# Attention stages of a four-layer kernel: one PSUM bank set aside for transposes, products of queries and keys drained by one copy, and small work moved to GpSimd

## The chip, the cores and the metric

The kernel runs on one NeuronCore of one Trainium2 chip. The metric is the device time of one execution in microseconds (us); the median of several runs is given, and the profile shows one further execution. Engines are named as in the profile: PE is TensorE (matrix products; PEld are its weight loads), DVE is VectorE, ACT is ScalarE, POOL is GpSimd, SP is SyncE, which here issues most of the DMAs.

## The reference

Four layers in turn on x of shape (1, 2048, 640): a Fourier layer, an attention layer, and both once more. Each adds its result to x.

```python
def _A_ref(x, seq_re, seq_im, hid_re, hid_im):        # Fourier layer
    a = einsum("bsd,ed->bse", x, hid_re); b = einsum("bsd,ed->bse", x, hid_im)
    return einsum("ts,bse->bte", seq_re, a) - einsum("ts,bse->bte", seq_im, b)

def _B_ref(x, wqkv, wo):                              # attention, 32 heads of 20, window of 256
    q, k, v = heads(x @ wqkv)
    scores = where(0 <= i - j < 256, q @ k.T * 20 ** -0.5, -1e9)
    return (softmax(scores) @ v) @ wo

x = x + _A_ref(layernorm(x), ...);  x = x + _B_ref(layernorm(x), ...)
x = x + _A_ref(layernorm(x), ...);  x = x + _B_ref(layernorm(x), ...)
```

Inputs and output are fp32. The kernel makes its large products from fp16 parts: each operand is a high part (the fp32 value rounded to fp16) and a low part (what is left, rounded again), and a product takes three matmuls, high by high, high by low and low by high.

## The kernel before

The program runs four stages: a spectral stage (Fourier layer), an attention stage, and both again. The change is in the attention stages; in the profile the first runs from about 602 to 1187 us, the second from about 1743 us to the end.

An attention stage goes through 256 steps `g`: 8 blocks of 256 queries, and 32 steps in a block, each for one tile of 128 queries and one pair of heads. What a step does is shifted against `g` by lags, counted in steps:

- at `g`, `scores(g)`: PE multiplies queries by keys into the bank `sp`; DVE masks it (COPY_PREDICATED, L1048) and takes the row maxima (TENSOR_REDUCE, L1052, into `m`; four steps share one `m`).
- at `HAND_LAG` (5) after the first step of each four, at the end of the step, `hand_on(n)`: the four steps' maxima are scaled and split into high and low parts in the tile `tops` (ACT L1058, then DVE L1059); four PE transposes put them into a PSUM bank, and two small ACT copies (L1067) put them into rows of `qs`, the stacked queries, so that the second product subtracts the maxima.
- at `KEY_LAG` (7), `by_key(g)`: PE multiplies keys by queries into the bank `tp`; ACT takes the sigmoid form of the exponential (L1088, into `ptq`); for every second pair POOL applies two triangular masks (L1093, L1095).
- at `VALUE_LAG` (12), `values(n)`: 32 PE matmuls of probabilities by values into `pv`, and one ACT copy. At `BACK_LAG` (14), `back(n)`: two PE transposes, DVE's division, and POOL's split (L1139, L1140) into `os`.

The banks `sp` and `tp` are single: a step's scores wait for the step before to be reduced.

Between these lies **filler work**, run by `run_fill`, which spends a credit of nanoseconds in each step (the rate is what is left of the filler over the steps that are left, times a factor `FILL` by the step's place among four). A filler unit is a generator that yields after each matmul. Kinds: products that make the next block's queries and keys (`Projections.qk`, 15 matmuls of 256 columns), values (`proj_v`) and outputs (`out_tile`, 15 of 320 columns), and **turns**: five transposes of a normed row tile or an output tile (`turned`), drained by one copy (ACT L952 for high parts, DVE L950 for low parts). A turn is taken by `step` in the middle of a product, after its seventh matmul, or by `run_fill` where no product is ready. `flush` runs to the end the units that the next block needs.

Products, turns and transposed maxima all take their bank from `new_f`, which hands out three banks in a fixed round: two of the pool `pf` and one of `p3`. A bank is free once the engine that drains it is done. A product of queries and keys is drained by two instructions, in line: ACT writes the high part (L328), then DVE reads the bank again, subtracts the high part, and writes the low part (L329); a DMA then stores both. Values are drained by ACT (L822), outputs by DVE (L877).

A layer norm in filler time (`norm_steps`, stepped by `slow_step`) runs on DVE, and ends with the normed tile `lny` (L147); `split` then has ACT make the high part (L159) and POOL the low part (L160) of `xs`.

All PE instructions of an attention stage keep the order of the code (`tensor` adds an order edge). The other engines' queues are put in order by the framework's scheduler, each engine runs its queue strictly in that order, and a waiting instruction holds all behind it.

Of the kernel before, what the change touches and what calls it, by code (L numbers as in the profile page):

```python
# [26 lines left out]
QB = 256  # L27
# [15 lines left out]
HAND_LAG = 5  # L43
KEY_LAG = 7
VALUE_LAG = 12
BACK_LAG = 14
# [12 lines left out]
def body(ctx: ExitStack, tc: tile.TileContext, x_in, cmat, whid, wqkv, wo, out):  # L59
# [18 lines left out]
    tops = [pers.tile([P, 4, 2, DH + 44], F16, name=f"tops{k}") for k in range(2)]  # L78
# [39 lines left out]
    def norm_steps(xs, ys):  # L118
# [26 lines left out]
        for k, x in enumerate(xs):  # L145
            y = keep.tile([P, D], F32, tag="lny", name="lny", bufs=2)
            normed[0] = nc.vector.tensor_scalar(y, x, mv[:, k, 0:1], g[:, k:k + 1],  # L147
                                                op0=OP.subtract, op1=OP.mult).ins
            ys.append(y)
            yield  # L150
# [142 lines left out]
    class Projections:  # L293


        def __init__(self):
# [7 lines left out]
            self.new_f = new_f  # L304
# [8 lines left out]
        def qk(self, b, w, ct):  # L313
            pf = self.new_f()
# [13 lines left out]
            nc.scalar.activation(t[:, 0], pf[:, :QB], AF.Copy, scale=down)  # L328
            nc.vector.scalar_tensor_tensor(t[:, 1], pf[:, :QB], down, t[:, 0], op0=OP.mult, op1=OP.subtract)  # L329
# [428 lines left out]
    def attention(layer, proj, dst, final):  # L758
        with ExitStack() as st:
# [14 lines left out]
            third = [0]  # L774
# [8 lines left out]
            proj.new_f = new_f  # L783
# [118 lines left out]
            def next_norm(i, x3):  # L902
                ys = []
                yield from norm_steps([x3], ys)
# [37 lines left out]
            def turned(xs, k, o, d0=0, d1=ND):  # L942
                pt = new_f()
# [43 lines left out]
            def step(u):  # L987

# [7 lines left out]
                if u.n % 15 == 7 and ns and not u.turn:  # L996
                    t = next_unit(True)
                    while t and step(t):
                        pass
                return True  # L1000

            def run_fill(ns):
                credit[0] += ns
                while credit[0] > 0:
                    if unit[0] is None:
                        unit[0] = next_unit(False) or next_unit()
                        if unit[0] is None:
                            credit[0] = 0.0
                            break
# [43 lines left out]

            def hand_on(n):

                b, q = divmod(n, NP // 2)
                m, hl = TOP.pop(n), tops[n % 2]
                nc.scalar.activation(hl[:, :, :, 0], m, AF.Copy, scale=-1.0 / M_UP)  # L1058
                nc.vector.scalar_tensor_tensor(hl[:, :, :, 1], m, -1.0 / M_UP, hl[:, :, :, 0], op0=OP.mult, op1=OP.subtract)  # L1059
                hp = new_f().bitcast(F16)[:, :4 * P].rearrange("p (a b) -> p a b", a=4)  # L1060
                for k in range(4):
                    transpose(hp[:66, k], hl[:, k].rearrange("p a b -> p (a b)")[:, :66], idh)
                for pi in range(2):
                    rs = slice(64 * pi, 64 * pi + 2)
                    o = QS[b][rs, 2 * q:2 * q + 2].rearrange("r p (i t) -> r i p t", i=2)
                    t = hp[rs].rearrange("r (i p) t -> r i p t", i=2)
                    nc.scalar.activation(o, t, AF.Copy)  # L1067
# [122 lines left out]
            for g in range(NS):  # L1190
# [12 lines left out]
                if g < NG and r == VALUE_LAG:  # L1203
# [7 lines left out]
                    if b == NBQ - 1 and not final:  # L1211
                        hidden = Hidden(xu_d)
                        hidden.load()
                        for k in range(2):
                            hidden.fetch(k)
                            fill.append(Unit(g + NEXT_STEPS[k], hidden.stage(k, None, new_f), "next", NG + k))
# [17 lines left out]
            while unit[0] is not None or fill or slow:  # L1234
                now[0] += 1
                run_fill(1600)
# [37 lines left out]
```

## Time and profile before

| | us |
|---|---|
| median of 3 runs | 2340.88 (2326.55 to 2344.01) |
| the profiled execution, its own time | 2334.45 |
| its span in the profile | 2332.7 |
| busy, of the span: PE / DVE / ACT / POOL | 92% / 73% / 55% / 51% |
| first and second attention stage | about 585 and 590 |

The engines run beside each other, so busy shares do not add up; the engine that is busy nearly all the time is PE, and what it waits for is what can be gained. The prediction is worked out against the profiled execution, 2334.45 us, which lies 0.3% below the median.

### The profile page before, as it was taken

To read this page: it belongs to the slowest core of one execution; us is meant where nothing else is said; L and a number is where in the kernel's file an instruction comes from. 1 tells how busy PE (TensorE), PEld (TensorE's weight loads), DVE (VectorE), ACT (ScalarE), POOL (GpSimd) and SP (SyncE) were. 2 spreads that over 40 slices of the span, in tenths; PEclk is the share of its full clock that TensorE was granted. 3 is DMA by queue.
4 is the path that set the end of the run, shared out by engine and by line. 5 is a ranking of instruction groups with operands and counts; after the bars stand their busy time and mean duration, and the time that the engine had idled before them with its cause. 6 is when DMAs were issued, how large, how long until landed. Compare 5 with 4: busy or idle time off the path is not lost.

```text
span 2332.7 us, 54695 instructions
## 1 busy us (share of the span) xinstructions
PE 2145.9 (92%) x21985; PEld 1504.6 (64%) x21985; DVE 1707.3 (73%) x3633; ACT 1290.8 (55%) x2248; POOL 1196.4 (51%) x1453
## 2 busy tenths in 40 slices
PE   7999899989899889999989999999898899999997
PEld 5667566667566666666556777777665666666664
DVE  7887969777668777776757858584767777677674
ACT  5334443333477677776764434334326677667675
POOL 5676757656134344443446858585642333334333
PEclk9999999999999999999999999999999999999999
DMA  5854646364421332232414535363642322232120
GB/s 185 290 208 155 217 144 208 133 226 132 133 79 44 95 90 64 59 96 70 155 70 154 193 130 191 128 214 148 227 116 70 87 60 67 67 87 75 54 76 24
DMA packets 187603, 292.93 MB, mean 126 GB/s; under 512 B 13908, under 2 KB 120660, under 8 KB 178004
## 3 DMA queue, kind: packets, MB, share of 16 engines
q1 hardware_dynamic: 157108, 223.55, 31.1%
q10 hardware_dynamic: 30240, 65.88, 7.6%
q8 instruction: 172, 2.82, 0.5%
q14 instruction: 83, 0.68, 0.1%
HBM read 202.51 MB, written 86.87 MB: 124 GB/s over the span
## 4 chain that ended last, share of the span: by engine, by line
PE 61%; DVE 21%; ACT 8%; DMA 5%; issue 4%; POOL 1%; SPq 0%; ACTq 0%; DVEq 0%; POOLq 0%
PE pf L112 26%; PE y L112 9%; PE pv L112 7%; PE z L112 6%; PE x L112 6%; DVE cc L481 5%; PE sp L112 4%; ACT ptq L1088 4%; DVE m L1052 3%; PE tp L112 3%; DVE sp L1048 2%; ACT qs L1067 2%; DVE res L504 1%; DVE early L329 1%; DVE lnst L125 1%
## 5 line engine op out<-in xcount | busy, mean ns | idle before, releaser
L112 PEld LDWEIGHTS <-cc 128*128 128x128 f16 x5376 | 527.6, 98 | 244.9 <-issue 37.8
L1088 ACT ACTIVATE ptq<-tp,shift,alpha 128x768 f32<-128x768 f32 (+2 forms) x512 | 487.0, 951 | 159.5 <-PE tp L112 134.1
L112 PEld LDWEIGHTS <-big 128*128 128x128 f16 x4320 | 411.6, 99 | 160.5 <-issue 47.7
L1093 POOL TENSOR_SCALAR_AFFINE_SELECT ptq<-ptq 128x512 f32<-128x512 f32 x224 | 144.3, 644 | 526.9 <-ACT ptq L1088 523.7
L1052 DVE TENSOR_REDUCE m<-sp 128x2 f32<-128x512 f32 (+1 forms) x512 | 345.1, 674 | 16.2
L112 PE MATMUL pf<-early,big 128*128 128x256 f16 x2400 | 316.2, 276 | 17.0 <-DVE early L329 16.9
L1048 DVE COPY_PREDICATED sp<-mask,sp 128x256 f32<-128x256 int32 x448 | 190.9, 426 | 162.3 <-PE sp L112 152.6
L478 ACT ACTIVATE cc<-cs 128x512 f16<-128x512 f32 x256 | 152.2, 623 | 256.6 <-POOL cs L471 99.9
L112 PE MATMUL y<-zc,cc 128*128 128x320 f16 x1728 | 268.2, 303 | 14.6 <-DVE pf L504 14.6
L112 PE MATMUL pf<-big 128*128 128x320 f16 x1680 | 241.7, 302 | 12.9 <-DVE early L250 7.4
L481 DVE SCALAR_TENSOR_TENSOR cc<-cs,cc 128x512 f16<-128x512 f32 x256 | 233.9, 929 | 3.6 <-ACT cc L478 3.6
L1095 POOL TENSOR_SCALAR_AFFINE_SELECT ptq<-ptq 128x512 f32<-128x512 f32 x256 | 164.9, 644 | 104.7 <-ACT ptq L1088 104.7
L481 DVE SCALAR_TENSOR_TENSOR cc<-cq,cc 128x512 f16<-128x512 f32 x192 | 203.4, 1060 | 0.0
L112 PE MATMUL pv<-ptq,v 128*32 128x128 f32 (+1 forms) x3840 | 185.9, 333 | 0.0
L112 PE MATMUL z<-zc,cc 128*128 128x320 f16 x1152 | 178.1, 299 | 5.6 <-DVE res L504 5.6
L112 PE MATMUL x<-zc,cc 128*128 128x320 f16 x1152 | 180.7, 301 | 0.0
L112 PE MATMUL sp<-ks,qs 62*128 62x256 f16 (+1 forms) x1792 | 153.9, 250 | 26.2 <-DVE m L1052 22.3
L112 PE MATMUL pf<-big,early 128*128 128x320 f16 x960 | 159.2, 301 | 7.8 <-DVE x L877 4.3
L112 PE MATMUL tp<-qs,ks 62*128 62x128 f16 x2688 | 151.0, 218 | 11.1 <-ACT ptq L1088 10.5
L1067 ACT ACTIVATE qs<-pf 2x512 f16<-2x512 f16 x224 | 131.2, 586 | 52.8 <-PE pf L112 47.2
L112 PE MATMUL pf<-bo,ot 128*128 128x320 f16 x840 | 146.3, 302 | 8.4 <-DVE x L877 3.7
L112 PEld LDWEIGHTS <-ks 62*128 62x128 f16 x3008 | 117.3, 95 | 54.2 <-issue 22.6
(140 smaller groups left out, 3383.8 us busy)
## 6 DMA issues: line engine op xcount, KB each, us to landing
cq<-in_cmat_dram SPq DMA_DIRECT2D x64, 1024.0 KB
accd<-res ACTq DMA_DIRECT2D x96, 320.0 KB
res<-accd SPq DMA_DIRECT2D x96, 320.0 KB
x<-x2d SPq DMA_DIRECT2D x64, 320.0 KB
qkd<-early SPq DMA_DIRECT2D x160, 128.0 KB
ks<-qkd SPq DMA_DIRECT2D x108, 160.0 KB
qs<-qkd SPq DMA_DIRECT2D x84, 160.0 KB
x2d<-res ACTq DMA_DIRECT2D x32, 320.0 KB
```

Source lines behind the costliest of these rows:

```text
L112: i = getattr(nc.tensor, what)(*args, **kw)
L125: nc.vector.bn_stats(st[:, h], x[:, h * 320:(h + 1) * 320])
L329: nc.vector.scalar_tensor_tensor(t[:, 1], pf[:, :QB], down, t[:, 0], op0=OP.mult, op1=OP.subtract)
L478: nc.scalar.activation(cc[m][:, 0], f, AF.Copy, scale=C_UP)
L481: nc.vector.scalar_tensor_tensor(cc[m][:, 1], f, C_UP, cc[m][:, 0], op0=OP.mult, op1=OP.subtract)
L504: marks["dve"] = nc.vector.scalar_tensor_tensor(o, z, Y_DOWN, f, op0=OP.mult, op1=OP.add).ins
L1048: nc.vector.copy_predicated(sp[:, :, 2 * P:3 * P], mask[:, None, :].to_broadcast([P, 2, P]), far)
L1052: topped[0] = nc.vector.tensor_reduce(TOP[g // 4][:, g % 4], sp[:, :, c0:3 * P], axis=AX.X, op=OP.max).ins
L1067: nc.scalar.activation(o, t, AF.Copy)
L1088: nc.scalar.activation(q[:, h:h + 2, a0 + first:a0 + 3], tp[:, :, first * P:3 * P].rearrange("p a (b c) -> p a b c", c=P), AF.Sigmoid, bia ...
L1093: nc.gpsimd.affine_select(out=q[:, :, a0], in_=q[:, :, a0], pattern=[[0, 4], [-1, P]], base=0, channel_multiplier=1, compare_op=OP.is_gt, ...
L1095: ins = nc.gpsimd.affine_select(out=q[:, :, a0 + 2], in_=q[:, :, a0 + 2], pattern=[[0, 4], [1, P]], base=0, channel_multiplier=-1, compare ...
```

## The change

Six edits, all for the attention stages (`Projections.qk` and `norm_steps` are also called at the end of the spectral stages):

1. `new_f` gives products the two banks of `pf` alone. The bank `p3` is kept for turns and transposed maxima, through `new_turn`.
2. A product of queries and keys is drained by one ACT copy to an fp32 tile `qf` in SBUF; POOL makes the high part (a cast) and the low part (a subtraction) from it.
3. The maxima are scaled, cast and subtracted on POOL (`part_tops`, three small instructions), in the middle of step `HAND_LAG`, now 4; `hand_on` at the end of that step only transposes; the two ACT copies are written in the code one and two steps later (`copy_tops`).
4. `norm_steps` of an attention stage writes the normed tile on POOL.
5. `VALUE_LAG` and `BACK_LAG` go from 12 and 14 to 13 and 15. The order of `FILL` moves with `VALUE_LAG`.
6. Turns are no longer taken inside products: `turn_unit` runs one whole turn ahead of the filler in the step of `hand_on` and in the step before it (two steps in four), and after the last scores in each step.

```diff
-HAND_LAG = 5
+HAND_LAG = 4
 KEY_LAG = 7
-VALUE_LAG = 12
-BACK_LAG = 14
+VALUE_LAG = 13
+BACK_LAG = 15
...
-            normed[0] = nc.vector.tensor_scalar(y, x, mv[:, k, 0:1], g[:, k:k + 1],
+            normed[0] = eng.tensor_scalar(y, x, mv[:, k, 0:1], g[:, k:k + 1],
...
-            nc.scalar.activation(t[:, 0], pf[:, :QB], AF.Copy, scale=down)
-            nc.vector.scalar_tensor_tensor(t[:, 1], pf[:, :QB], down, t[:, 0], op0=OP.mult, op1=OP.subtract)
+            f = keep.tile([P, QB], F32, tag="qf", name="qf", bufs=2)
+            nc.scalar.activation(f, pf[:, :QB], AF.Copy, scale=down)
+            nc.gpsimd.tensor_copy(t[:, 0], f)
+            nc.gpsimd.tensor_tensor(t[:, 1], f, t[:, 0], op=OP.subtract)
...
-            def new_f():
-
-                third[0] += 1
-                if third[0] % 3 or not in_turn[0]:
-                    return pf_.tile([P, 512], F32, tag="f", name="pf", bufs=2)
-                return p3.tile([P, 512], F32, tag="f", name="pf")
+            def new_turn():
+
+                return p3.tile([P, 512], F32, tag="f", name="pt") if in_turn[0] else new_f()
...
-                yield from norm_steps(x2s, ys)
+                yield from norm_steps(x2s, ys, nc.gpsimd)
...
-                pt = new_f()
+                pt = new_turn()
...
-                if u.n % 15 == 7 and ns and not u.turn:
-                    t = next_unit(True)
-                    while t and step(t):
-                        pass
+            def turn_unit():
+                t = next_unit(True)
+                while t and step(t):
+                    pass
...
-                        unit[0] = next_unit(False) or next_unit()
+                        unit[0] = next_unit(False)
...
+            def part_tops(n):
+
+                m, hl = TOP.pop(n), tops[n % 2]
+                u = sb.tile([P, 4, 2], F32, tag="u", name="u", bufs=2)
+                nc.gpsimd.tensor_scalar(u, m, -1.0 / M_UP, None, op0=OP.mult)
+                nc.gpsimd.tensor_copy(hl[:, :, 0:66:64], u)
+                nc.gpsimd.tensor_tensor(hl[:, :, 1:66:64], u, hl[:, :, 0:66:64], op=OP.subtract)
+
             def hand_on(n):
 
-                b, q = divmod(n, NP // 2)
-                m, hl = TOP.pop(n), tops[n % 2]
-                nc.scalar.activation(hl[:, :, :, 0], m, AF.Copy, scale=-1.0 / M_UP)
-                nc.vector.scalar_tensor_tensor(hl[:, :, :, 1], m, -1.0 / M_UP, hl[:, :, :, 0], op0=OP.mult, op1=OP.subtract)
-                hp = new_f().bitcast(F16)[:, :4 * P].rearrange("p (a b) -> p a b", a=4)
+                hl = tops[n % 2]
+                hp = new_turn().bitcast(F16)[:, :4 * P].rearrange("p (a b) -> p a b", a=4)
...
+                if (g - HAND_LAG) % 4 in (0, 3) or g >= NG + HAND_LAG:
+                    turn_unit()
                 run_fill(max(rate, 400) * FILL[(g - VALUE_LAG + 2) % 4])
```

What it does to the order of PE, at the end of a step that hands maxima on, is seen at two places of the first attention stage. Before, step 89 (`bo`, `ot`: an output product; `os`: a turn of an output tile; `tops_78`: the maxima); the turn stands in the middle of a product, and the maxima directly behind it, each in a bank of its own:

```order
L112 MATMUL pf<-bo_66,ot 128x320
L112 LDWEIGHTS os
L112 MATMUL pf<-idh,os 128x128
...
L112 LDWEIGHTS tops_78
L112 MATMUL pf<-idh,tops_78 66x128
...
L112 LDWEIGHTS qs
```

After the change, step 96, the first of a block, in which no filler has credit:

```order
L112 MATMUL tp<-qs,ks 128x128
L112 LDWEIGHTS os
L112 MATMUL pt<-idh,os 128x128
...
L112 LDWEIGHTS tops_78
L112 MATMUL pt<-idh,tops_78 66x128
...
L112 LDWEIGHTS qs
```

The turn has moved to right behind the second product `tp`, and both now write the same bank, `pt`. Of the 128 times that maxima are handed on, 41 have a turn ahead of them in the same step (37 before, and then in other banks); in 12 of the 41 nothing stands between, in the other 29 there is a product's share of 1280 to 3840 columns, 2240 in the middle one.

On POOL, in the first attention stage, the new work (`qf` and `early`: a product's copy and its parts; `u` and `tops`: the maxima) stands between the masks of `ptq` and the split of `os`:

```order
L1097 AFFINE_SELECT ptq<-ptq 128x4x128
L1099 AFFINE_SELECT ptq<-ptq 128x4x128
L329 CAST early<-qf 128x256
L330 TENSOR_TENSOR early<-qf,early 128x256
L1053 TENSOR_SCALAR u<-m 128x8
L1054 CAST tops_78<-u 128x4x2
L1055 TENSOR_TENSOR tops_78<-u,tops_78 128x4x2
L1143 CAST os<-o 128x2x80
L1144 TENSOR_TENSOR os<-o,os 128x2x80
```

None of the rows from `qf` to `tops` was in POOL's queue before. For all but the first of each stage, the masks ahead of `u` are those of the products two steps before the step that hands on.

More of the change, by code (lines that the diff above doesn't have):

```diff
@@ L77, in body @@
     ones = pers.tile([P, 2, 2 * NP * QB // P], F16, name="ones")
-    tops = [pers.tile([P, 4, 2, DH + 44], F16, name=f"tops{k}") for k in range(2)]
+    tops = [pers.tile([P, 4, 66], F16, name=f"tops{k}") for k in range(2)]
     def constants():
@@ L1215, in attention @@
                             hidden.fetch(k)
-                            fill.append(Unit(g + NEXT_STEPS[k], hidden.stage(k, None, new_f), "next", NG + k))
+                            fill.append(Unit(g + NEXT_STEPS[k], hidden.stage(k, None), "next", NG + k))
+                for pi in range(2):
+                    n, m = divmod(g - HAND_LAG - 1 - pi, 4)
+                    if m == 0 and 0 <= n < NG // 4:
+                        copy_tops(n, pi)
+                n, m = divmod(g - HAND_LAG, 4)
+                if m == 0 and 0 <= n < NG // 4:
+                    part_tops(n)
                 slow_step()
```

25 lines of the change are left out of this document (12 added, 13 removed).

## The prediction

> **What bounds the kernel now.** I read the page first, for the engine that sets the time, then the busy time of each engine in the two attention stages, then what PE waits for there.
>
> ```profile
> PE 2145.9 (92%) x21985; PEld 1504.6 (64%) x21985; DVE 1707.3 (73%) x3633; ACT 1290.8 (55%) x2248; POOL 1196.4 (51%) x1453
> PE   7999899989899889999989999999898899999997
> 601.70:1186.70 585.00, 528.80 (x6921) 366.07 (x6922) 446.68 (x1150) 417.85 (x677) 228.30 (x406) 0.99 0.30 84
> 1743.20:2333.00 589.80, 534.11 (x6979) 363.55 (x6978) 403.40 (x964) 408.02 (x657) 216.42 (x406) 0.99 0.24 67
> ```
>
> The columns of the last two rows are PE, PEld, DVE, ACT, POOL, the granted clock and the DMA share. PE is nearly always busy, in the attention stages too, and its clock is 0.99 of full: the change alters no matmul, so it can only fill PE's gaps, 585.0 - 528.8 = 56 us and 589.8 - 534.1 = 56 us. What ends these gaps is in the list of waits of PE, for each stage:
>
> ```profile
> PE pf L112 <- DVE early L329: 17.3, 14, 2.5
> PE sp L112 <- DVE m L1052: 16.5, 30, 1.6
> PE pf L112 <- DVE x L877: 6.6, 8, 2.0
> PE pf L112 <- ACT v L822: 5.0, 6, 1.3
> PE tp L112 <- ACT ptq L1088: 3.1, 7, 0.8
> ...
> PE sp L112 <- DVE m L1052: 15.7, 32, 1.3
> PE pf L112 <- DVE early L329: 12.6, 12, 1.9
> PE pf L112 <- DVE x L877: 7.3, 7, 3.7
> PE tp L112 <- ACT ptq L1088: 6.0, 16, 1.0
> PE pf L112 <- ACT v L822: 2.3, 2, 1.4
> ```
>
> The rows are the total in us, the times, and the longest. The waits on `pf` are waits for a **bank**: 17.3 + 12.6 for the drain of queries and keys, 6.6 + 7.3 for that of outputs, 5.0 + 2.3 for that of values, 51 us together. The waits of `sp` for L1052 (32 us) and of `tp` for L1088 (9 us) are of another kind: the two single banks of scores.
>
> How a bank wait arises is seen in the timeline of the first stage:
>
> ```profile
> 850.38 0.34 PE L112 MATMUL sp<-ks,qs 62*128 62x256 f16 x4
> 850.56 0.33 PE L112 MATMUL tp<-qs,ks 62*128 62x128 f16 x6
> 850.93 0.99 ACT L1088 ACTIVATE ptq<-tp,shift,alpha 128x768 f32<-128x768 f32 x1 [0.47 <-PE tp L112]
> 851.23 0.69 DVE L1052 TENSOR_REDUCE m<-sp 128x2 f32<-128x512 f32 x1
> 852.03 0.44 PE L112 MATMUL pf<-idh,xs 128*128 128x128 f16 x5
> 852.51 0.70 ACT L952 ACTIVATE xto<-pf 128x640 f16<-128x640 f16 x1 [0.32 <-PE pf L112]
> 852.71 0.38 PE L112 MATMUL pf<-idh,tops 128*66 128x128 f16 x4 [0.23 <-DVE early L329]
> 853.73 1.04 PE L112 MATMUL pf<-early,big 128*128 128x256 f16 x8
> 855.23 0.37 ACT L328 ACTIVATE early<-pf 128x256 f16<-128x256 f32 x1
> 855.64 0.42 DVE L329 SCALAR_TENSOR_TENSOR early<-pf,early 128x256 f16<-128x256 f32 x1 [0.53 <-ACT early L328]
> 856.12 0.49 PE L112 MATMUL pf<-early,big 128*128 128x256 f16 x3 [1.34 <-DVE early L329]
> ```
>
> A turn (852.03) and the maxima (852.71) took two of the three banks of the round; so the product that began at 856.12 got the bank of the product that had just ended, and waited 1.34 us for its two drains one behind the other.
>
> **Edit 1 and 2, the banks.** With two banks for products alone, a product waits for the one before the last, and that has the time of a whole product to drain: 15 matmuls at 1.04/8 = 0.13 us, 2.0 us. The ACT drain is late by at most one L1088, 0.99 + 0.37 = 1.4 us; the DVE drain of outputs, which stays, by one mask, one reduction and itself.
>
> ```profile
> L877 DVE SCALAR_TENSOR_TENSOR x<-pf,beta,x 128x320 f32<-128x320 f32 x56 | 30.1, 539 | 10.3 <-PE pf L112 10.0
> L1048 DVE COPY_PREDICATED sp<-mask,sp x448: 404/429/434, 662.5 to 2302.6; 128x256 f32<-128x256 int32 x150
> ```
>
> That is 0.43 + 0.69 + 0.54 = 1.7 us. Both are under 2.0, so I leave 3 us of the 51: **48 us** of waits go. They do not all become time. From 850.38 to the end of the reduction at 851.92 are 1.54 us, and the next scores cannot start earlier; the step was short enough to wait for that 30 + 32 times, and 7 + 16 times for L1088, 85 waits in 512 steps, one step in six. A PE that comes earlier meets these more often. I let a quarter come back: **-36 us** (bounds -48 and, if all came back, 0).
>
> **DVE is lighter.** It loses L329, the split of the maxima, and the normed tile (here of the first stage; the second has 70, 64 and 12):
>
> ```profile
> L329 DVE SCALAR_TENSOR_TENSOR early<-pf,early 128x256 f16<-128x256 f32 x70 | 29.6, 424 | 22.7 <-ACT early L328 20.8 <-DMA ks<-qkd 0.7 <-DMA x<-x2d 0.3
> L1059 DVE SCALAR_TENSOR_TENSOR tops<-m,tops 128x8 f16<-128x8 f32 x63 | 16.2, 256 | 7.5 <-ACT tops L1058 7.4
> L147 DVE TENSOR_SCALAR lny<-x,lnmv,lnt 128x640 f32<-128x640 f32 x25 | 17.3, 704 | 0.1
> ```
>
> These are 63 us of 447, and near 55 of 403 in the second stage: 14%. But the wait of `sp` for L1052 mostly follows from a step that is shorter than 1.54 us, which a lighter DVE does not alter. Bounds 0 and -32; I take 14% of it, **-4 us**. ACT loses its 64 small scalings of the maxima in each stage and keeps everything else.
>
> **Edits 1, 3 and 6, one bank for turns and maxima.** Here the change adds a wait on PE: where a turn precedes the maxima in the same step (41 times, 12 of them directly), the transposes of the maxima wait for the turn's copy, and all of PE waits behind them. Before, they had two banks, as this place shows, where the copy begins after the maxima have begun:
>
> ```profile
> 862.87 0.44 PE L112 MATMUL pf<-idh,os 128*128 128x128 f16 x5 [0.65 <-DVE early L329]
> 863.15 0.39 PE L112 MATMUL pf<-idh,tops 128*66 128x128 f16 x4
> 863.35 0.49 DVE L950 COPY ot<-pf 128x640 f16<-128x640 f16 x1 [0.53 <-PE pf L112]
> ```
>
> The turn now stands right behind `tp`, so its copy queues behind the step's reduction (DVE, 1.54 + 0.49 = 2.0 us after the step's start) or behind its L1088 (ACT: 851.92 - 850.38 + 0.70 = 2.2 us). Where nothing stands between, the maxima were wanted 0.8 us after the start, but the next scores not before 1.54: with 0.25 us for the transposes themselves the next scores are at 2.3 to 2.5, about 0.9 late, of which the emptied step behind it returns something: 0.5 us, 12 times, 6 us. With the middle gap of 2240 columns at 0.5 ns (1.04 us for 2048) they are wanted at 0.8 + 1.1 = 1.9 us and get the bank at 2.05 to 2.3: 0.3 us, 29 times, 9 us. Together **+15 us** (bounds 0, where ACT and DVE come early, and 41 times 1.0).
>
> **POOL's new work.** For a cast and a subtraction of 256 columns, three tiny operations and a normed tile the nearest rows are these:
>
> ```profile
> L1139 POOL CAST os<-o 128x160 f16<-128x160 f32 x60 | 20.1, 335 | 20.6 <-DVE o L1137 17.0 <-DVE lnt L133 3.6
> L1140 POOL TENSOR_TENSOR os<-o,os 128x160 f16<-128x160 f32 x60 | 29.3, 489 | 4.7
> L160 POOL TENSOR_TENSOR xs<-lny,xs 128x640 f16<-128x640 f32 x25 | 35.1, 1409 | 13.4 <-ACT xs L159 13.3
> L809 POOL MEMSET v<- 128x11 f32 x32 | 3.7, 118 | 0.0
> L1095 POOL TENSOR_SCALAR_AFFINE_SELECT ptq<-ptq 128x512 f32<-128x512 f32 x256 | 164.9, 644 | 104.7 <-ACT ptq L1088 104.7
> ```
>
> A subtraction grows by (1409 - 489)/480 = 1.9 ns a column: 0.67 us at 256. The cast lies between 0.34 (no growth) and 0.54 (all growth); I take 0.42. A normed tile lies between 0.7 (the DVE row) and 1.4 (L160); I take 1.0. Each tiny one lies between 0.12 (the memset) and 0.34; I take 0.2. In the first stage 70 x 1.09 + 28 x 1.0 + 64 x 0.6 = 143 us, POOL goes from 228 to 371 of 585 us (63%); in the second 76 + 12 + 38 = 126, to 342 of 590 (58%). A rule speaks against this move: in the Trainium skill, "GPSIMD Engine Reference", section "4.1 Engine selection", elementwise work belongs on VectorE, and two-input work takes GpSimd about twice as long. The rows bear the ratio out (1409 ns for L160's 640 columns in two inputs, 704 for L147's in one). By that page's 2.6 cycles an element at 1.2 GHz (section "3.1 Elementwise — side-by-side cycle accounting"), an estimate of 0.55 us for 256 columns, the 143 us would be 135, and the sum of the terms the same; slower it would be only by the third rival below.
>
> POOL has the time; the question is lateness. The maxima are ready 1.54 us into a step of 585/256 = 2.28, 0.74 before the step that hands them on, and PE wants them 1.9 us into it: after 0.6 us of POOL's three, 2.0 us are left (0.9 in the twelve bare places). Ahead in POOL's queue stand the masks of two steps earlier (2 x 0.64) and at times a product's parts (1.1) or a normed tile. Two of these must come late together; one time in ten by 0.5 us is **+6 us** (bounds 0, and 128 times 1 us).
>
> ACT's high part of a normed tile (L159) now waits for POOL, with L1088 of the next steps behind it, and `tp` behind that; ACT has 167 of 585 us idle, which hides most: **+3 us** for 40 of them (bounds 0 and 40). The copy `qf` has two buffers, so ACT waits for POOL only when it is two products late. The stores of queries and keys, on SP's queue, leave about 1 us later; the wait of `sp` for these loads was at most this in a stage, so nothing is added:
>
> ```profile
> PE sp L112 <- DMA qs<-qkd: 0.6, 1, 0.6
> ```
>
> **Lags and order.** One step more to the values hides POOL's later masks, and puts the last values one step later, behind which filler still stands. The order has six more steps without filler in the last blocks, each short of 1.54 us by 0.7 or so: with that, **+4 us**. The ten products that end each spectral stage are drained the new way too; PE ran without a gap beside them, and I count nothing:
>
> ```profile
> 540.00:570.00 30.00, 30.00 (x246) 23.78 (x244) 22.73 (x49) 7.77 (x17) 13.01 (x11) 1.00 0.47 142
> ```
>
> **The sum**: -36 - 4 + 15 + 6 + 3 + 4 = -12 us on 2334.45. The added waits were each taken at the full price, as though PE had nothing to catch up with; where two fall into one step they are paid once, for which I take off 3: **2319 us**, 0.7% under the profiled execution and 0.9% under the median. About 1% is what a measurement of this kernel can tell from no change.
>
> **Rivals.**
> *The whole gain.* The copies of turns come before the maxima want their bank, and a lighter DVE shortens the waits of `sp`: -48, half of -32, and +7 for the lags and POOL, -57: 2277; with some of it, up to 2305. For it: the drains are short (0.37 to 0.70 us), and ACT and DVE are idle for a quarter of the stage. Against it: the turn's new place, right behind `tp`. Chance 0.23.
> *The third bank takes the place of the other two.* 41 collisions at 1.0 us, and half the gain comes back: -24 + 41 - 4 + 10 = +23 if all, so 2325 to 2355. Against it: only 41 of 128. Chance 0.13.
> *POOL comes late, and PE waits for the maxima* (slower). Place: the transposes of `tops`; PE stands, and everything with it. The point from which it decides is 2.0 us of lateness; each further 0.5 us costs up to 128 x 0.5 = 64 us. With 1 us over in half of the 128, 64 us against a gain of 36 + 4 and the 19 of collisions and lags: +43, 2377. What would do it: a normed tile and a low part (1.0 + 1.4 us) in front of the maxima, or rows that run longer than I took them. Against it: such pairs come 40 times, not 128. Chance 0.14.
>
> **How the numbers follow.** My forecast, 2305 to 2340, has 0.50, of which 0.16 is below 2311 (1% under the profiled execution). Faster by over 1%: 0.23 + 0.16 = 0.39. Slower by over 1% (2358): the last rival and the end of the one before it, 0.17. Between, 0.44. The range leaves out the ends of the first and the last rival, about 0.08 below and 0.12 above: 2285 to 2356.
>
> **What the profile after would show.** Waits of `pf` for L328, L817 or L872 near 3 us in sum, and none for POOL: step one right. A new row, `pt` waiting for L945 or L947 (the turn's copies), near 15 us, and PEld or `pt` waiting for POOL's `tops`, near 6: the added terms. L1052's row as before, near 30. DVE down by some 120 us, POOL up by some 270. It would be wrong if `pf` still waited 20 us or more, or if `tp` waited for L1088 by over 20 us, with ACT held up by POOL ahead of it.

## The result, and the profile after

The changed kernel takes **2401.02 us** (median of 4 runs, 2394.44 to 2404.99), the kernel before 2334.31 us on the same chip: a ratio of **1.0281** (95% interval 1.0227 to 1.0334). It is 2.8% slower, where 0.7% faster was forecast. In g1, one of the experiments below, the profiled execution ran at a granted clock of 0.794 and took 2628.96 us, so its ratio leaves this execution out and its trace is not set beside the others.

From the page of the changed kernel:

```profile
span 2403.3 us, 55464 instructions
...
PE 2169.1 (90%) x21985; PEld 1515.7 (63%) x21985; DVE 1621.3 (67%) x3305; ACT 1267.7 (53%) x2120; POOL 1539.1 (64%) x2197
```

The busy time in stretches of 613.6 and 612.2 us of its two attention stages (PE, PEld, DVE, ACT, POOL, granted clock, DMA share, GB/s):

```profile
605.80:1219.40 613.60, 536.83 (x6892) 367.38 (x6891) 399.59 (x976) 405.30 (x611) 397.38 (x759) 0.96 0.28 78
1790.80:2403.00 612.20, 541.67 (x6979) 369.35 (x6978) 367.27 (x818) 396.65 (x593) 356.19 (x750) 0.96 0.24 64
```

The span grew by 2403.3 - 2332.7 = 70.6 us. PE runs the same 21985 matmuls; 2169.1 - 2145.9 = 23 us of the growth is PE busy longer, at a lower granted clock (0.96 in the stretches, 0.99 before), and 47 us are new gaps. DVE lost 86 us and POOL gained 343: the work moved as intended.

What PE waits for in the first stretch (total, times, longest):

```profile
PE sp L112 <- DVE m L1047: 17.7, 21, 2.3
PE tp L112 <- ACT ptq L1092: 15.7, 15, 3.5
PE pt L112 <- POOL tops L1055: 9.6, 9, 2.0
PE pt L112 <- ACT xto L947: 7.3, 5, 3.4
PE pt L112 <- DVE ot L945: 6.3, 5, 1.7
...
PE pf L112 <- DVE x L872: 0.6, 1, 0.6
...
PE pf L112 <- ACT qf L328: 0.3, 1, 0.3
```

The bank waits on `pf` are gone: 0.6 and 0.3 us here, where L329 and L877 had 17.3 and 6.6 (their lines are now L328 and L872). In their place stand waits on the shared bank `pt`, for the copies of turns (L945, L947) and for POOL's maxima, and a wait of `tp` for the sigmoid copy (L1092, before L1088), over five times its 3.1 us. The waits of the whole run name what stands behind that:

```profile
ACT xs L159 <- POOL lny L147: 69.7, 36, 4.6
...
PE tp L112 <- ACT ptq L1092: 37.6, 27, 4.4
...
ACT xs L159 <- DVE lny L147: 34.0, 14, 4.5
```

ACT's high part of a normed tile (L159) waits 69.7 us for POOL. Here is what that does to PE, from the timeline of the first stage:

```profile
957.32 0.38 ACT L1125 ACTIVATE pvs<-pv 128x256 f32<-128x256 f32 x1
...
957.59 0.33 PE L112 MATMUL tp<-qs,ks 62*128 62x128 f16 x6
...
957.95 5.02 POOL L147 TENSOR_SCALAR lny<-x,lnmv,lnt 128x640 f32<-128x640 f32 x2
...
960.50 0.74 ACT L159 ACTIVATE xs<-lny 128x640 f16<-128x640 f32 x1 [2.81 <-POOL lny L147]
...
961.15 0.98 ACT L1092 ACTIVATE ptq<-tp,shift,alpha 128x768 f32<-128x768 f32 x1
...
962.17 0.34 PE L112 MATMUL tp<-qs,ks 62*128 62x128 f16 x6 [2.02 <-ACT ptq L1092]
```

At 957.70 ACT is free, and `tp` is complete at 957.92. But next in ACT's queue is L159, and the tile that it reads begins on POOL only at 957.95. ACT stands 2.81 us, L1092 begins at 961.15, over 3 us after its input was there, and PE stands 2.02 us at the next `tp`. The groups of POOL's new work (busy us, mean ns of one) give the reason:

```profile
L330 POOL TENSOR_TENSOR early<-qf,early 128x256 f16<-128x256 f32 x160 | 109.1, 682 | 10.9
...
L147 POOL TENSOR_SCALAR lny<-x,lnmv,lnt 128x640 f32<-128x640 f32 x40 | 102.3, 2560 | 15.6 <-DVE lnt L143 14.9
...
L329 POOL CAST early<-qf 128x256 f16<-128x256 f32 x160 | 66.8, 417 | 20.9 <-ACT qf L328 20.8
...
L1053 POOL TENSOR_SCALAR u<-m 128x8 f32<-128x8 f32 x128 | 31.0, 242 | 85.6 <-DVE m L1047 76.3 <-DVE lnt L132 2.7 <-DVE lnt L141 2.2
```

The normed tile takes **2.56 us** on POOL, where DVE took 0.70. The other new rows are near the sizes that the prediction took.

### The profile page after: what moved, and what is told of

Read it like the earlier page. It is cut to its first block, busy times and chain, and to the rows that moved or that the text cites. A ratio compares the mean times of both kernels' runs of the same rounds, so it can differ in the third digit from the quotient of the medians.

```text
span 2403.3 us, 55464 instructions
## 1 busy us (share of the span) xinstructions
PE 2169.1 (90%) x21985; PEld 1515.7 (63%) x21985; DVE 1621.3 (67%) x3305; ACT 1267.7 (53%) x2120; POOL 1539.1 (64%) x2197
## 4 chain that ended last, share of the span: by engine, by line
PE 58%; DVE 17%; POOL 9%; DMA 7%; issue 5%; ACT 3%; SPq 0%; DVEq 0%; ACTq 0%; POOLq 0%
PE pf L112 23%; PE y L112 8%; PE pv L112 6%; PE z L112 6%; PE x L112 6%; DVE cc L482 5%; PE sp L112 4%; POOL lny L147 3%; DVE m L1047 2%; PE tp L112 2%; PE pt L112 2%; DVE sp L1043 2%; ACT ptq L1092 2%; DMA x<-x2d 1%; DVE res L505 1%
## 5 line engine op out<-in xcount | busy, mean ns | idle before, releaser
L112 PEld LDWEIGHTS <-cc 128*128 128x128 f16 x5376 | 528.0, 99 | 243.4 <-issue 38.8
L1092 ACT ACTIVATE ptq<-tp,shift,alpha 128x768 f32<-128x768 f32 (+2 forms) x512 | 486.2, 950 | 212.5 <-PE tp L112 199.5
L112 PE MATMUL y<-zc,cc 128*128 128x320 f16 x1728 | 265.3, 301 | 13.7 <-DVE pf L505 13.7
L112 PE MATMUL pv<-ptq,v 128*32 128x128 f32 (+1 forms) x3840 | 191.2, 340 | 0.0
L1069 ACT ACTIVATE qs<-pt 2x512 f16<-2x512 f16 x224 | 131.4, 586 | 54.1 <-PE pt L112 50.4
L112 PEld LDWEIGHTS pv<-ptq,v 128*32 128x32 f32 x3840 | 110.4, 113 | 59.9 <-issue 8.2
```

The costliest lines, as they stand in the source:

```text
L112: i = getattr(nc.tensor, what)(*args, **kw)
L1069: nc.scalar.activation(o, handed[n][rs].rearrange("r (i p) t -> r i p t", i=2), AF.Copy)
L1092: nc.scalar.activation(q[:, h:h + 2, a0 + first:a0 + 3], tp[:, :, first * P:3 * P].rearrange("p a (b c) -> p a b c", c=P), AF.Sigmoid, bia ...
```

## The experiments

Two questions were put. Is edit 4 (the normed tile on POOL) the loss, and if so by what: ACT standing in its queue (call it A1), or POOL's load or the instruction itself? And why was there nothing left of the bank gain without it? Each ratio is to the kernel before, measured beside it on the same chip, with its 95% interval. The groups of runs were taken on several chips, so runs of different groups are compared by their ratios.

### Edit 4 undone, and edit 4 alone

**e1_norm_dve**, the changed kernel with the normed tile back on DVE:

```diff
...
-                yield from norm_steps(x2s, ys, nc.gpsimd)
+                yield from norm_steps(x2s, ys)
```

> The changed kernel with one edit undone: the normed tile of the attention stages is written by VectorE again. Theory A (the normed tile on GpSimd is the cause: 40 executions of 2.56 us, ACT waits 62 us for them in the attention stages, PE waits for ACT and the clock drops): most of the 67 us comes back, 2315 to 2345 us, and the waits of tp for L1092 fall from 36 us to under 15. Rival B (the shared third bank and the turns' new place are the cause): 2375 to 2395 us. Rival C (GpSimd as a whole is too busy): half comes back, 2350 to 2375 us.

Measured 2339.82 us, 1.0026 (1.0010 to 1.0042), as theory A has it: of the 2.8%, edit 4 is 2.6. The wait of `tp`, 37.6 us in the changed kernel, is nearly gone:

```profile
PE tp L112 <- ACT ptq L1092: 3.6, 10, 1.0
```

**b4_norm_pool**, the kernel before with edit 4 alone:

> The kernel before with that one edit alone: the normed tile of the attention stages on GpSimd. Theory A: 40 to 65 us slower than before, 2375 to 2400 us, with ACT waiting some 60 us for the normed tile. Rival B: within 10 us of before. Rival C: 10 to 25 us slower, since GpSimd is otherwise little loaded here.

Measured 2405.32 us, 1.0304 (1.0285 to 1.0323), 5 us over theory A's range: one edit on 40 instructions costs 3%. The page's PE row, then two waits, and the second of them in the kernel before:

```profile
PE 2177.0 (90%) x21985; PEld 1517.5 (63%) x21985; DVE 1686.9 (70%) x3593; ACT 1291.8 (54%) x2248; POOL 1292.0 (54%) x1493
```

```profile
ACT xs L159 <- POOL lny L147: 80.7, 35, 7.4
...
PE tp L112 <- ACT ptq L1088: 53.4, 37, 4.6
```

```profile
PE tp L112 <- ACT ptq L1088: 10.7, 25, 1.0
```

The span grew by 75.3 us (2408.0 against 2332.7). PE's wait of `tp` for L1088 was 10.7 us in the whole run before: 42.7 of the 75 are that wait, and 31 are PE busy longer (2177.0 - 2145.9) at a granted clock of 0.970 instead of 0.986. ACT stood for DVE's tile before, too: 55.9 us in the whole run, of which 32.6 are left in b4. So some 23 us of standing became 81.

### Is it POOL's load? The other two moves undone

**e3_drain_old** (the drain of queries and keys by ACT and DVE, as before) and **e2_maxima_old** (the maxima split on ACT and DVE) are the changed kernel with one more edit undone each. The edit of e3:

```diff
-            f = keep.tile([P, QB], F32, tag="qf", name="qf", bufs=2)
-            nc.scalar.activation(f, pf[:, :QB], AF.Copy, scale=down)
-            nc.gpsimd.tensor_copy(t[:, 0], f)
-            nc.gpsimd.tensor_tensor(t[:, 1], f, t[:, 0], op=OP.subtract)
+            nc.scalar.activation(t[:, 0], pf[:, :QB], AF.Copy, scale=down)
+            nc.vector.scalar_tensor_tensor(t[:, 1], pf[:, :QB], down, t[:, 0], op0=OP.mult, op1=OP.subtract)
```

> The changed kernel with the drain of queries and keys undone (ACT and then VectorE read the bank, no work of GpSimd). Theory A: little changes, 2390 to 2410 us, since the normed tile stays. Rival C: GpSimd is 175 us lighter, 2360 to 2385 us. If the drain by one copy was worth what the prediction said, some bank waits come back, at most 10 us with two banks for products.

> The changed kernel with the scaling and splitting of the maxima on ACT and VectorE again. Theory A: the waits of PE for GpSimd's tops (15 us on pt, more on the weight loads) go, but they come mostly behind a normed tile, and ACT is still held by it: 2380 to 2395 us. Rival B: no change. Rival C: 2370 to 2385 us.

Measured 2364.93 (1.0131, 1.0116 to 1.0146) and 2383.44 (1.0214, 1.0192 to 1.0237). e3 lies in rival C's range and 25 us under theory A's: with 1.1 us of POOL's work gone from each product 1.5% (35 us) come back, though the normed tile stays on POOL. Of its waits against those of the changed kernel, ACT's for the tile falls only from 69.7 to 62.8 us, PE's of `tp` from 37.6 to 30.8, of `pt` for `tops` from 15.0 to 5.8, and of `sp` from 38.8 to 31.4; so POOL's load is a second cost beside ACT's standing. The same edit gives 0.95% back where the tile is on DVE (e8, below); that the rest goes with the tile in POOL's queue is likely, but not shown. e2 lies in the ranges of both theory A and rival C and does not tell them apart.

**b6_pool_idle_work**, the kernel before, in which POOL writes each normed tile a second time, into a tile that nobody reads:

```diff
+            if also:
+                z = also.tile([P, D], F32, tag="lnz", name="lnz")
+                nc.gpsimd.tensor_scalar(z, x, mv[:, k, 0:1], g[:, k:k + 1], op0=OP.subtract, op1=OP.mult)
```

> The kernel before, in which GpSimd writes each normed tile of the attention stages a second time, into a tile that nobody reads; VectorE's is used as before. Theory A1 (ACT waits in its strict order for the tile, and that is the cost): within 15 us of before, since ACT waits for VectorE's tile as before. Rival A2 (GpSimd's queue is late by 2.56 us for masks and low parts, whoever writes the tile that counts): 30 us or more over before, with PE waiting for ptq or xs of GpSimd.

Measured 2346.8, 1.0056 (1.0038 to 1.0074), within A1's 15 us. The same 40 instructions ran on POOL, and PE's wait of `tp` stayed (10.7 before):

```profile
L152 POOL TENSOR_SCALAR lnz<-x,lnmv,lnt 128x640 f32<-128x640 f32 x40 | 102.9, 2573 | 45.3 <-DVE lnt L143 43.5 <-DMA ks<-qkd 0.5 <-DVE tops L1062 0.3
```

```profile
PE tp L112 <- ACT ptq L1091: 11.6, 27, 1.0
```

The load itself is 0.6%. What makes 3% of it is that somebody waits for the result.

### The bank gain, without edit 4

e1 has the new banks and still gains nothing. Its waits of PE:

```profile
PE sp L112 <- DVE m L1047: 35.9, 50, 2.3
...
PE pt L112 <- DVE ot L945: 12.6, 10, 2.0
PE pt L112 <- POOL tops L1055: 10.5, 9, 2.7
...
PE pt L112 <- ACT ot L947: 8.2, 14, 1.3
PE pt L112 <- ACT xto L947: 6.2, 9, 1.3
PE pt L112 <- DVE xto L945: 6.0, 7, 2.6
```

With two more rows (4.1 and 3.8), `pt` waits 41 us for copies of turns. By the timeline 25.4 of them, in 37 waits, are the transposes of the maxima; the other 15.5 are turns that wait for the turn before them. **e5_turn_later** is e1 with the turns taken out of the step that hands the maxima on; they run in the two steps before it:

```diff
-                if (g - HAND_LAG) % 4 in (0, 3) or g >= NG + HAND_LAG:
+                if (g - HAND_LAG) % 4 in (2, 3) or g >= NG + HAND_LAG:
```

**e7_turn_later_maxima_old** and **e8_turn_later_drain_old** are e5 with edit 3's split, or edit 2, undone as above; **e9_banks_only** with both, so that only banks, lags and turns are moved; **e11_banks_turn_as_changed** is e9 with the turns where the change put them.

> The changed kernel with the normed tile on VectorE and the turns moved: they run in the two steps before the one that hands the maxima on (2 and 3 after the last), none in that step itself. Theory B1 (what the two product banks gain is lost to the 41 us that the transposes wait for turns' copies in the shared third bank): those waits fall under 15 us, and the time to 2295 to 2315 us. Rival B2 (a wait that goes comes back as another, since VectorE's and ACT's chain sets the step): 2325 to 2340 us.

> As the kernel with turns moved and the normed tile on VectorE, and the maxima scaled and split by ACT and VectorE. If the 10 us that PE waits for GpSimd's tops are a cost of their own: 8 to 12 us under that kernel. If ACT's and VectorE's two more instructions cost as much: the same within 5 us.

> As the kernel with turns moved and the normed tile on VectorE, and the queries' and keys' bank drained by ACT and then VectorE as before. Theory: two banks for products alone already give the time to drain, so the one-copy drain is worth under 5 us, and a GpSimd that is 175 us lighter and a VectorE that is 59 us heavier about cancel: within 8 us of that kernel. If the one copy is what removes the bank waits: 15 us or more slower.

> Only the banks, the lags and the turns of the change, the turns two and one step before the one that hands the maxima on; the normed tile, the maxima and the drain of queries and keys as in the kernel before. If the 7 us of the maxima and the 21 us of the drain add up: 2276 to 2284 us. If they pay for the same waits: 2284 to 2292 us.

> As the last, with the turns where the change puts them (in the step that hands the maxima on, and the one before). Theory (the shared third bank costs where the turn's copy stands ahead of the maxima): 20 to 35 us over the last kernel, as from 2307 to 2340 with the other edits in, with some 40 us of waits of pt. Rival (that loss needed GpSimd's load): within 10 us of it.

| run | us | ratio | interval |
|---|---|---|---|
| e5 | 2307.42 | 0.9890 | 0.9867 to 0.9914 |
| e7 | 2300.18 | 0.9849 | 0.9828 to 0.9871 |
| e8 | 2286.46 | 0.9795 | 0.9773 to 0.9816 |
| e9 | 2289.91 | 0.9789 | 0.9768 to 0.9810 |
| e11 | 2318.40 | 0.9909 | 0.9892 to 0.9926 |

The turn's place is worth 1.36% (e1 to e5) and 1.2% (e11 to e9), as theory B1 has it. In e11 the six rows of `pt` waiting for L943 and L945 are 39.9 us, in e9 15.2; the maxima's share of them falls from 24.3 to 1.5. The one-copy drain, edit 2, does not pay: from e5 to e8 21 us come back, where at most 8 were expected in either direction. POOL's cast and subtraction stand ahead of the maxima, and PE's wait of `pt` for them falls by 9.7 us; its wait of `sp` for the reductions falls by as much (50.5 to 41.3), for a reason that was not looked for. The first two rows are of e5, the last two of e8:

```profile
PEld L112 <- POOL tops L1055: 18.0, 19, 3.0
...
PE pt L112 <- POOL tops L1055: 12.7, 14, 2.6
```

```profile
PEld L112 <- POOL tops L1053: 6.2, 12, 1.4
...
PE pt L112 <- POOL tops L1053: 3.0, 8, 1.2
```

The savings of e7 (7 us) and e8 (21) do not add up in e9, which by its ratio is no faster than e8 within the intervals: both pay for the same lateness of the maxima, of which e8 leaves only 3.0 us in `pt`. **e8 and e9 beat both kernels**, by 2.1% against the one before (intervals 1.8 to 2.3%).

### Does ACT's standing cost it, or the instruction?

**e10_normed_and_high_on_pool** is e9 with the normed tile and its high and low part all on POOL, so that ACT has no part in it:

```diff
-        nc.scalar.activation(hi, y, AF.Copy)
+        if both:
+            eng.tensor_copy(hi, y)
+        else:
+            nc.scalar.activation(hi, y, AF.Copy)
```

> As the kernel with only banks, lags and moved turns, but GpSimd writes the normed tile, its high part and its low part one behind the other, so that ACT waits for nothing of it. Theory A1 (the damage of the normed tile on GpSimd was ACT's wait in its strict order): within 20 us of that kernel, though GpSimd has 40 times 2.56 us and a cast more. Rival A2 (GpSimd's late queue): 40 us or more over it.

Measured 2303.94, 0.9851 (0.9832 to 0.9870): 14 us over e9, where the tile alone cost b4 70, with POOL's 2.5 us instruction in place and even more work behind it; the wait is gone:

```profile
PE tp L112 <- ACT ptq L1091: 4.1, 13, 1.0
```

The next runs keep ACT's part and ask for it later. **c2_split_later** (the kernel before, DVE's tile), **f2_norm_pool_later** (b4), **f3_after_later** (the changed kernel) and **f4_best_norm_pool_later** (e9 with edit 4) write the split two steps later, at both places (the lines are f3's):

```diff
                 yield from norm_steps([x3], ys, nc.gpsimd)
+                yield
+                yield
                 xs = new_xs()
```

> The kernel before, with the split of a normed tile issued two steps (about 4.6 us) after the norm instead of one; nothing on GpSimd. A control for the next three: the order of fillers shifts a little with it. Both theories: within 10 us of the kernel before, ratio 0.996 to 1.004.

> The kernel before with the normed tile on GpSimd (1.0304 alone, 70 us) and the split three steps behind the norm instead of one, so that ScalarE is asked for the high part some 6.9 us after GpSimd's 2.5 us instruction was issued. Theory A1 (the price is ScalarE standing in its queue for this tile, with the score copies behind it): most of the 70 us goes, 2335 to 2355, and PE's wait of tp for the score copies falls from 53 us to under 20. Rival (GpSimd's instruction itself costs: its port, its load, its clock): the time stays, 2390 to 2410.

> The changed kernel with the split of a normed tile three steps behind the norm instead of one; the tile stays on GpSimd. Theory A1: close to the run with the tile back on VectorE, 2335 to 2365, PE's wait of tp for the score copies under 15 us (37.6 in the changed kernel). Rival (GpSimd's instruction itself costs): 2390 to 2405.

> The best version so far (only banks, lags and turns moved, 0.9789) with the normed tile on GpSimd and its split three steps behind the norm. If GpSimd's tile costs nothing once nobody stands in a queue for it, the lighter VectorE shows: 2280 to 2292. If its 1.4 us low parts come late for the turns, or the load counts, 2300 to 2320.

| run | us | ratio | interval |
|---|---|---|---|
| c2 | 2346.73 | 1.0052 | 1.0032 to 1.0071 |
| f2 | 2414.74 | 1.0339 | 1.0304 to 1.0375 |
| f3 | 2431.36 | 1.0421 | 1.0378 to 1.0464 |
| f4 | 2369.97 | 1.0148 | 1.0106 to 1.0190 |

The control c2 is 10 us slower, and its ratio a little over what was expected. f2 and f3 lie over even the rival's ranges, and f4 is 80 us over e9 and 50 over its own. But the wait that they were to take away was still there, as f2's rows show, and a place in its timeline:

```profile
ACT xs L159 <- POOL lny L147: 89.9, 37, 7.4
...
PE tp L112 <- ACT ptq L1092: 50.6, 45, 4.3
```

```profile
851.48 2.49 POOL L147 TENSOR_SCALAR lny<-x,lnmv,lnt 128x640 f32<-128x640 f32 x1
...
854.01 0.74 ACT L159 ACTIVATE xs<-lny 128x640 f16<-128x640 f32 x1 [2.71 <-POOL lny L147]
```

The order of ACT's queue explains it: no score copy stands between the tile and L159, though the code asks for L159 three steps after the tile. The scheduler, which orders all engines but PE, put L159 ahead of copies that stand before it in the code. So f2 to f4 did not test A1. **g1_norm_pool_split_pinned** (f2) and **g4_best_norm_pool_pinned** (f4) hold L159 behind the score copy of its step by an order edge on ACT; POOL's instructions are the same:

```diff
-                split(xs[:, 0], xs[:, 1], ys[0], nc.gpsimd)
+                with tc.issue_after(shown[0]):
+                    split(xs[:, 0], xs[:, 1], ys[0], nc.gpsimd)
...
-                nc.scalar.activation(q[:, h:h + 2, a0 + first:a0 + 3],
+                shown[0] = nc.scalar.activation(q[:, h:h + 2, a0 + first:a0 + 3],
...
```

> The kernel before with the normed tile on GpSimd, its split three steps behind the norm, and now an order edge that keeps ScalarE's high part (L159) behind the score copy of the step in which it is written; without that edge the scheduler had put it three score copies ahead of its place in the code, so that ScalarE still stood 89.9 us for it. Theory A1 (ScalarE standing in its queue is the price): ScalarE's wait for the tile falls from 80.7 and 89.9 us to under 30 over the run, PE's wait of tp for the score copies from 53 and 51 to under 20, and the time to 2335 to 2360 (1.000 to 1.010, the control c2 being 1.005). Rival (GpSimd's instruction itself costs: a shared port, load, clock): 2395 to 2415 with the wait gone.

> The version with only banks, lags and turns moved (0.9789), with the normed tile on GpSimd, the split three steps behind the norm and pinned behind the score copy as in g1. Theory A1: 2285 to 2315 (f4, which lacked the pin, 2370), PE's wait of tp for the score copies under 15 us (42 in f4). Rival: 2355 to 2375.

g1: 2353.66, 1.0066 (1.0044 to 1.0089), in A1's range. Against f2's 1.0339, 2.7% come back by an order edge alone, and what is left is the control's 1.0052 within the intervals; on this base POOL's instruction costs nothing measurable once nobody stands for it. A control with the edge and DVE's tile was not run, so what the edge does by itself is not known. g4: 2318.04, 0.9925 (0.9907 to 0.9943), 3 us over the range given for A1, against 2370 for f4. The waits of f4, then of g4:

```profile
ACT xs L159 <- POOL lny L147: 58.9, 37, 3.5
...
PE tp L112 <- ACT ptq L1092: 42.1, 36, 4.8
```

```profile
ACT xs L159 <- POOL lny L147: 13.2, 6, 3.5
...
PE tp L112 <- ACT ptq L1094: 8.8, 13, 2.2
```

On e9's base A1 is shown by the time and by the waits, on the base of the kernel before by the time; on the changed kernel itself it rests on e1. Nor is VectorE slowed by POOL's instruction, another way in which it could cost by itself: the mean of its wide reductions is 0.691 us in the kernel before and in b4, and 0.690 in g4. By the ratios g4 still stands 1.4% (some 32 us) behind e9. Its trace shows where part of this is: around 1235 us, at the end of the first attention stage, PE stands 8.0 and 3.4 us for L159, which it does not in e9, and `pt` waits 9.8 us for the turns' copies to `early` by ACT, 0.8 in e9. Edit 4 paid in none of these runs.

### Why 2.5 us?

**m1_forms** is e9 with eight GpSimd instructions at the start, one of each form, for their durations:

```python
...
nc.gpsimd.tensor_scalar(b, a, s, s, op0=OP.subtract, op1=OP.mult)              # L93: two row scalars
...                                                                            # L94: the same on 320 columns
nc.gpsimd.tensor_scalar(b, a, s, None, op0=OP.subtract)                        # L95: one row scalar
nc.gpsimd.tensor_scalar(b, a, 1.0, 2.0, op0=OP.subtract, op1=OP.mult)          # L96: two constants
nc.gpsimd.tensor_scalar(b, a, 2.0, None, op0=OP.mult)                          # L97: one constant
nc.gpsimd.tensor_copy(b, a)                                                    # L98
nc.gpsimd.tensor_tensor(b, a, a, op=OP.subtract)                               # L99
```

> The same kernel with eight more instructions of GpSimd at the start, read one by one for their duration (its time is not read): a memset of 128x640, then 128x640 (once 128x320) in fp32 from SBUF to SBUF: two operations with a scalar for each row, one with it, two with constants, one with a constant, a copy, and a subtraction of two tiles. If the scalar per row makes the normed tile cost 2.5 us: only the forms with it are over 1.5 us. If it is two operations: the form with two constants too. If it is the size: the copy too.

The groups of POOL by form (busy us, mean ns of the one):

```profile
L93 POOL TENSOR_SCALAR form<-form,shift 128x640 f32<-128x640 f32 x1 | 2.5, 2507 | 0.0
L96 POOL TENSOR_SCALAR form<-form 128x640 f32<-128x640 f32 x1 | 2.4, 2437 | 0.1
L95 POOL TENSOR_SCALAR form<-form,shift 128x640 f32<-128x640 f32 x1 | 1.9, 1897 | 0.1
L97 POOL TENSOR_SCALAR form<-form 128x640 f32<-128x640 f32 x1 | 1.8, 1818 | 0.1
L94 POOL TENSOR_SCALAR form<-form,shift 128x320 f32<-128x320 f32 x1 | 1.4, 1435 | 0.1
L99 POOL TENSOR_TENSOR form<-form 128x640 f32<-128x640 f32 x1 | 1.2, 1249 | 0.0
L98 POOL COPY form<-form 128x640 f32<-128x640 f32 x1 | 1.2, 1201 | 0.1
```

It is the operations, not the operands: a copy is 1.20 us, one operation with a constant 1.82, two 2.44, and row scalars instead of constants add 0.07 to 0.08. From 320 to 640 columns the form of the normed tile grows by 3.35 ns a column. Each form ran once.

## Why the prediction was wrong, point by point

**The banks: right, and worth more than taken.** 48 us of waits on `pf` were to go; e1 has 3.7 us left for outputs (`pf` for L872) and none for the drains of queries, keys and values. A quarter was to come back on `sp` and `tp`. But with only the banks, the lags and moved turns, e9, the kernel is 2.1% faster, 49 us against the 36 taken, and `sp` and `tp` wait 35.3 and 5.9 us there, 32.2 and 10.7 before. In the change itself hardly any of it became time, because of the next terms.

**The shared bank: right in kind, mis-sized.** The term was +15 us at 0.3 to 0.5 us a collision. In the change the transposes of the maxima wait 28.6 us for copies of turns, 35 times, 0.8 us each, and the turn's place is worth 28 to 32 us. Turns that wait for turns, the other 15 us of e1's 41, were not priced; e9 keeps 13.7 of them. The rival "the third bank takes the place of the other two" had 41 collisions at 1.0 us, and its range, 2325 to 2355 (its own sum of +23 would make that 2357), holds e1's 2339.8; but that both 41s agree is chance.

**POOL late for the maxima, +6 us: mis-sized too.** In the change `pt` waits 15.0 us for `tops`. What POOL does for the maxima and the products together costs 1.0% (24 us, e5 against e9) or 1.2% (27 us, e1 against e11). The rival on the slower side (2377) had the right engine and the wrong place: not PE at `tops`, but ACT at the normed tile. With the maxima back on ACT and DVE, e2 still measured 2383. The forecast's sum without edit 4 was -18 us, and e1 is +5: the runs share this out as -49 for banks and lags (e9), +28 for the turn's place (e11), and +27 for POOL's part of edits 2 and 3 (e1 against e11), together +6.

**DVE lighter, -4 us: not borne out.** DVE lost 86 us, where some 120 were forecast, and `sp` waits 38.8 us for the reductions in the change and 35.9 in e1, 32.2 before. The +4 for lags and order was not measured by itself.

**POOL's new work: one row wrong, and the rest follows from it.** The cast (0.42 taken, 0.417 measured), the subtraction (0.67 and 0.682) and the tiny ones (0.2; 0.21 to 0.24) came as worked out. The normed tile was taken at 1.0 us, between DVE's 0.7 and the 1.4 of L160, and took 2.56, outside both bounds. The error was to bound one form by another: L160 is a single subtraction, L147 two operations on a row scalar each, and no row of the trace before showed a POOL instruction of that form at this size. POOL gained 343 us, not 270; 62 of the difference are the 40 normed tiles at 1.56 us more than taken. The ratio that the prediction read off its rows set POOL's two-input row beside DVE's one-input row; the trace before has one DVE row of L160's form, 0.82 us, against which POOL's 1.41 is 1.7 times as long. The Trainium skill ("GPSIMD Engine Reference", section "4.1 Engine selection") calls one-input elementwise work on GpSimd roughly line-rate; here the normed tile, with one tensor input and two operations, took 2.56 us, over three times DVE's 0.70, so the measurement decides.

**"ACT waits for POOL's normed tile", +3 us: this is the step that failed.** Edit 4 cost 2.6%, some 60 us (e1 against the change). It was priced as a share of ACT's idle time, 167 of 585 us. But idle time in the mean hid next to nothing here, since the queue is strict: ACT stands at L159 while the score copy behind it has its input, and PE needs `tp` back within the step. With the tile at 2.56 us, behind masks and products' parts on POOL, ACT stood 69.7 us. The bound of 40 us was also too low, since it counted one microsecond a tile and not the lower clock. The text had named this under what would make it wrong: `tp` waiting for L1088 by over 20 us, with ACT held up by POOL; it is 37.6.

**Not foreseen:** PE busy 23 us longer on the same matmuls, at a lower granted clock. Two windows of the changed kernel (PE busy is the first number after the length, the granted clock the third from the end), the first around the place shown above, where PE stood 2.02 us at 962.17, the second around one where it stood 2.14 us at 1171.63:

```profile
960.00:970.00 10.00, 6.46 (x96) 4.28 (x91) 4.29 (x9) 7.09 (x11) 9.61 (x16) 1.00 0.14 48
1170.00:1180.00 10.00, 6.70 (x79) 4.01 (x78) 3.63 (x8) 6.80 (x10) 5.13 (x10) 0.66 0.98 408
```

The clock dropped at one of them and not at the other, and at the second the DMA engines were busy nearly all the time as well (0.98). Over the whole execution it is lower in the change (0.970) and in b4 (0.970) than before (0.986), and 0.984 in e10 and 0.981 in g4, where the gaps go; but e1, without them, has 0.971 to 0.981 in its ten executions. What lowers the clock stays open.

## What to carry to other kernels

Before moving an instruction to a slower engine, look at who reads its result and what stands behind that reader in its own queue: 40 instructions that cost 0.6% as idle load cost 3% as something that ScalarE, in strict order, had to stand for. Take the duration from a row of the same form, operations counted, or measure it; a neighbour by size is no bound. And a bank that is set aside must not be asked for twice in one step: the same banks gave 2.1% (e9) with the turns in the two steps before the maxima and 0.9% (e11) with a turn in front of them in the same step.

## What the runs showed of the hardware

A GpSimd TENSOR_SCALAR on 128 x 640 fp32 costs by its operations: 1.82 to 1.90 us with one, 2.44 to 2.56 with two (m1, and the normed tile in the change), against 1.20 for a copy and 0.70 for the two-operation form on VectorE (the mean of 25 in the first attention stage before). And the wait of PE was not all that b4 paid: of its 75 us, 43 are the wait itself and 31 are the same matmuls, longer at a granted clock of 0.970 instead of 0.986; whether the one brought the other was not tested.
